# A linear-attention block with a GEGLU feed-forward: K^T V formed from tokens^T phi(K), and folded into the output weights

## The chip, the cores and the metric

The kernel runs on one core of a Trainium2 chip. The metric is device time in microseconds (us), as the median of several runs. All activations and weights are bf16, matmuls accumulate in f32 in PSUM (8 banks of 512 f32 a partition).

## What is computed

One token block of 2048 tokens, model width 448, 16 heads of 28, feed-forward width 1792 (a batch of one):

```python
def _A_ref(x, wqkv, wo):                      # x is layernorm(tokens)
    q, k, v = (x @ wqkv) split in three, 16 heads of 28
    phi = lambda t: jnp.where(t > 0, t + 1, jnp.exp(t)) + 1e-6
    pq, pk = phi(q), phi(k)
    kv = jnp.einsum("bhsd,bhse->bhde", pk, v)
    z = jnp.einsum("bhsd->bhd", pk)
    num = jnp.einsum("bhqd,bhde->bhqe", pq, kv)
    den = jnp.einsum("bhqd,bhd->bhq", pq, z)[..., None] + 1e-6
    return (num / den) put back to [S, 448] @ wo
...
h = x + _A_ref(_layernorm(x), A_wqkv, A_wo)
h2 = h + (gelu(n @ w_gate) * (n @ w_up)) @ w_down      # n = _layernorm(h)
```

## The kernel before

The 2048 tokens are 16 tiles of 128. A small graph class collects tasks (one task is one engine instruction or one run of matmuls) with the buffers that they read and write; from these it derives the semaphore waits. The order of the tasks on each engine is not found at run time: `ORDERS` is a table of five lists of task numbers (TensorE, ScalarE, VectorE, GpSimd, and SyncE with the DMAs that it issues). Each engine works through its list strictly in order, so a task that waits holds up all that stand behind it on its engine.

**First layernorm.** For each tile VectorE computes `bn_stats` and `bn_aggr` (L421, L422), ScalarE the reciprocal deviation as exp(-0.5 ln(var)) (L431, L433), and the normalised tile `xn` comes from VectorE (tiles 0 and 1, L458) or GpSimd (the rest, L461). It is transposed to `xnT` on TensorE for tiles 0 to 3 (L483 to L486), and by DMA transposes on SyncE's queue for tiles 4 to 15 (L494). Width 448 is three blocks of 128 rows and one of 64; the 64 are doubled by a copy (L467), so that the half block can be used from both halves of the array.

**K, V and the state.** Tiles go in pairs. K and V of a tile are three matmuls each over 128 rows (L513, L521) and one each over 64 rows; the two half matmuls (L524, L525) run at once in the two halves of the array. phi(K) takes three steps: ScalarE's exp out of PSUM (L539), GpSimd's clamp (L545), VectorE's max-and-add out of PSUM (L547). ScalarE copies V out (L549). Then four matmuls per tile (L555), 113 columns each, add phi(K)^T V in PSUM, four heads to a group, with a column of ones for z. After the last tile VectorE masks the blocks off the diagonal (L566, L567) into `kvz`.

**Q.** It is made transposed, 113 rows by 512 tokens at a time (L580, 16 pieces of four matmuls), and phi(Q) goes the same way: L583 on ScalarE, L584 on GpSimd, L585 on VectorE.

**Attention out, `a2_tile`.** Per tile: four matmuls give numerators and denominators at once (`nd`, L603); VectorE takes the reciprocals (L606) and multiplies (L607) into `o_sb`; that is transposed (tiles 0 and 1 on TensorE, L617; then DMA, L622); the output projection (`wo`, L630; in pairs L640 with two half matmuls L641, L642); VectorE adds the residual (L651); the second layernorm follows, with GpSimd's power (L438, L440) and normalisation (L665) from tile 2 on; the wide copy (L685); and the transposes to `hnT` (L675 on TensorE for tiles 0 and 1, then DMA, L686).

**Feed-forward.** `gu_chunk` takes 2, 2, 4, 4 and 4 tiles. Gate and up are 64-row matmuls in the two halves of the array, side by side (L741, L743), seven to a column block; ScalarE applies gelu (L765), VectorE multiplies (L767). `b2_tile` does the down projection, 14 matmuls per tile (L702), and VectorE adds the residual (L707). Gate uses PSUM banks 0 and 1, up 6 and 7, down 2 and 3, so that a gate/up step can run two ahead of VectorE and no more. There are 56 such steps, called gu0 to gu55 below; the first is issued when both tiles of the first chunk have their `hnT`. The order lists put the attention of tiles 4 and later between the gate/up steps, and the last Q pieces between the steps of the chain that leads to the first gate/up.

Of the kernel before, what the change touches and what calls it, by code (L numbers as in the profile page):

```python
# [5 lines left out]
BF16 = mybir.dt.bfloat16  # L6
F32 = mybir.dt.float32
ALU = mybir.AluOpType
AF = mybir.ActivationFunctionType

ENGS = ("pe", "act", "dve", "pool", "sp")
SEM_LAT = {"pe": 0.05, "act": 0.05, "dve": 0.05, "pool": 0.12, "sp": 0.06}
DMA_ISSUE = 0.45
DMA_LAT = 1.6
T0 = 0.8
CONTEND = 3.9
DMA_BW = 300e3
MODE_SWITCH = 0.1
MODE_HYST_64 = 1.2
MODE_HYST_128 = 0.0  # L20
MODE_MIN_64 = 2.5

# [3 lines left out]
    "30 43 36 152 153 145 59 51 146 159 160 246 151 171 158 172 165 250 170 183 184 177 254 182 195 196 189 207 194 208 201"  # L26
    " 258 206 220 221 213 232 219 233 226 262 231 266 238 270 243 274 313 310 278 282 316 318 343 340 290 320 286 326 294 298"
    " 348 302 334 364 338 367 306 413 418 423 428 433 438 372 443 391 388 448 478 483 396 488 493 457 454 451 498 503 462 508"
    " 543 548 553 519 522 513 516 527 558 563 628 625 568 573 578 583 633 588 593 598 603 608 652 649 616 613 657 673 678 683"
    " 688 693 698 703 619 622 708 713 718 723 728 733 738 743 746 755 760 765 770 775 780 785 790 795 800 805 810 815 820 749"  # L30
    " 752 825 828 831 834 837",
    "3 5 6 7 29 33 34 40 41 56 57 48 49 157 66 67 52 60 150 154 147 79 80 161 166 164 247 169 118 92 105 93 106 181 176 178"
    " 173 251 119 131 132 190 185 188 255 193 197 200 202 205 218 214 212 259 209 225 215 222 230 227 234 237 239 263 242 267"
    " 271 275 279 283 317 319 291 287 324 325 295 299 330 331 303 335 307 412 416 414 421 419 424 426 431 429 436 434 441 439"
    " 444 446 479 481 486 484 491 489 494 496 501 499 506 504 509 511 546 544 554 549 556 551 559 561 564 566 571 569 576 574"
    " 581 579 586 584 591 589 594 596 601 599 609 606 611 604 676 674 679 681 684 686 691 689 696 694 704 699 701 706 711 709"
    " 714 716 721 719 726 724 731 729 739 741 736 734 756 758 763 761 768 766 771 773 778 776 783 781 788 786 793 791 796 798"
    " 801 803 808 806 811 813 818 823 816 821",
    "19 20 31 32 38 39 35 53 42 45 44 54 46 61 37 63 62 64 100 74 87 115 69 113 76 75 72 77 114 156 88 101 149 116 89 102 82"
    " 85 128 90 103 163 249 168 108 126 95 98 127 129 175 253 111 180 187 192 124 121 137 199 257 204 134 211 217 224 229 261"  # L40
    " 236 241 265 244 245 269 314 311 315 312 277 273 281 341 344 342 345 321 285 322 327 323 328 289 329 332 293 333 336 349"
    " 337 352 297 339 350 351 368 301 353 417 415 365 354 366 422 420 369 425 427 362 432 430 359 305 309 435 442 437 440 376"
    " 373 377 374 445 378 375 389 447 390 392 393 386 480 482 485 397 487 398 400 401 402 399 383 449 455 490 492 456 458 497"
    " 495 459 407 410 500 502 507 505 466 510 512 463 547 545 452 464 467 555 557 520 465 521 523 524 552 550 517 528 531 529"
    " 532 560 562 530 533 626 565 468 567 629 627 572 570 630 577 575 514 582 538 580 473 585 541 587 476 592 590 595 597 634"
    " 602 600 637 653 650 651 612 605 610 654 635 614 607 636 638 658 659 677 675 617 680 682 661 685 687 692 690 697 660 695"
    " 662 663 639 620 702 700 644 707 647 668 705 712 710 715 717 671 623 722 720 727 725 732 730 740 742 735 737 757 759 764"
    " 762 769 767 772 774 779 777 784 782 789 787 794 792 797 799 802 804 747 809 807 744 812 814 822 819 817 824 750 753 826"
    " 829 832 835 838",
    "16 18 24 25 23 27 0 21 17 22 55 47 28 58 50 65 68 71 26 155 148 78 81 84 167 162 248 91 104 107 94 97 117 179 174 252"  # L50
    " 110 130 136 191 123 186 120 133 256 198 203 216 260 210 223 228 235 240 264 268 272 276 280 284 288 292 296 300 308 356"
    " 357 304 355 361 358 380 381 379 385 382 404 405 403 409 406 535 534 470 469 536 540 471 472 537 475 641 642 665 640 664"
    " 666 646 667 643 670",
    "1 2 4 8 9 10 11 12 13 14 15 70 73 83 86 96 99 109 112 122 125 139 135 141 138 140 143 142 346 347 144 371 370 360 363"
    " 394 395 387 384 460 461 411 408 525 526 631 632 450 542 474 515 539 477 655 656 615 648 621 669 453 672 618 645 754 830"
    " 751 748 827 624 518 745 836 833 839",
)


class _Buf:  # L60
    __slots__ = ("name", "writer", "readers")

    def __init__(self, name):
        self.name = name
        self.writer = None
        self.readers = []

# [4 lines left out]


class _Graph:


    def __init__(self):
        self.all = []
# [131 lines left out]
def bass_sequential_preLN__linear_attn_block__glu_gated_geglu__prompt_kernel(  # L210
# [4 lines left out]
    T = S // 128  # L215
# [625 lines left out]
```

## Time and profile before

| what | value |
|---|---|
| median of 3 runs | 203.81 us (202.98 to 204.15) |
| span of the profiled execution | 201.6 us, 2.2 us less than the median; the page gives no other time of that execution |
| first K matmul | 8.57 us into the span |
| first gate/up matmul | 58.72 us |
| end of the last matmul | about 199.1 us |
| busy: TensorE, VectorE, ScalarE, GpSimd | 194.9, 119.4, 70.4, 53.0 us |
| granted TensorE clock, mean | 0.992 of full speed |
| DMA transposes | 12 of `xn`, 14 of `o_sb`, 14 of `hn`, median 2.5, 2.5 and 3.0 us from issue to landing |

How to read it. The busy time of TensorE is modelled: a matmul counts from its start to the end of its flow through the array, so neighbours overlap. What a run of matmuls costs is read from start to start in the timeline. The same holds in a smaller way for the other engines: a row says how long one instruction took, and a run of like instructions takes somewhat less each. A digit in the line of 40 slices is the busy share of a slice of 5.04 us in tenths.

### The profile page before, as it was taken

How to read it: one execution, taken by the hardware profiler on the slowest of the kernel's cores; microseconds unless marked ns; L12 is line 12 of the kernel's file. 1: busy time of each engine (PE TensorE's matmuls, PEld its weight loads, DVE VectorE, ACT ScalarE, POOL GpSimd, SP SyncE). 2: the span in 40 equal slices, each digit the busy share in tenths (PEclk: the TensorE clock that was granted, in tenths of full speed). 3: DMA queues.
4: the chain of work that ended last, by engine and by line, in shares of the span. 5: the costliest groups of instructions: out<-in, count | busy, mean ns of one | idle time of the engine just before them, and what ended most of it. 6: DMA issues, size and time to landing. Idle time of an engine off the chain costs nothing.

```text
span 201.6 us, 4406 instructions
## 1 busy us (share of the span) xinstructions
PE 194.9 (97%) x1684; PEld 110.4 (55%) x1684; DVE 119.4 (59%) x312; ACT 70.4 (35%) x191; POOL 53.0 (26%) x105
## 2 busy tenths in 40 slices
PE   7599999799999999999999999999999999999995
PEld 7245455356578767675544445456444545555554
DVE  2877653369997875946657666564553324573112
ACT  3257556366564312222213232043032224432000
POOL 8349994344416050500006300003600000000000
PEclk9979999999999999999999999999999999999999
DMA  6942425999980613260111285100078000000014
GB/s 187 364 78 54 81 53 116 141 262 280 181 300 19 121 37 72 59 134 3 26 26 29 51 162 72 49 2 3 0 138 117 0 0 3 0 0 3 23 62 143
DMA packets 38276, 17.39 MB, mean 86 GB/s; under 512 B 29808, under 2 KB 37360, under 8 KB 38256
## 3 DMA queue, kind: packets, MB, share of 16 engines
q1 hardware_dynamic: 36832, 14.71, 34.0%
q10 hardware_dynamic: 1424, 2.41, 4.3%
q8 instruction: 13, 0.21, 0.4%
q14 instruction: 7, 0.06, 0.1%
HBM read 8.66 MB, written 1.84 MB: 52 GB/s over the span
## 4 chain that ended last, share of the span: by engine, by line
PE 90%; DMA 5%; SPq 2%; issue 1%; DVE 1%; ACT 0%; DVEq 0%
PE ps L741 36%; PE ps L702 21%; PE ps L743 7%; PE ps L580 7%; PE ps L640 4%; PE ps L513 4%; PE ps L521 4%; DMA xnT<-xn 3%; DMA x_sb<-in_A_x_dram 2%; PE ps L603 2%; PE ps L524 2%; PE ps L555 1%; SPq L494 1%; PE ps L641 1%; PE ps L630 1%
## 5 line engine op out<-in xcount | busy, mean ns | idle before, releaser
L743 PE MATMUL ps<-hnT,wgu_sb 64*128 64x512 bf16 (+1 forms) x490 | 87.3, 334 | 0.0
L741 PE MATMUL ps<-hnT,wgu_sb 64*128 64x512 bf16 (+1 forms) x490 | 86.9, 334 | 0.0
L765 ACT ACTIVATE gl<-ps 128x256 bf16<-128x256 f32 x112 | 36.5, 382 | 86.9 <-PE ps L743 83.3
L767 DVE TENSOR_TENSOR hh<-ps,gl 128x256 bf16<-128x256 f32 x112 | 42.5, 416 | 38.7 <-ACT gl L765 37.8
L741 PEld LDWEIGHTS ps<-hnT,wgu_sb 64*128 64x128 bf16 x490 | 45.4, 94 | 29.0 <-issue 1.5
L743 PEld LDWEIGHTS ps<-hnT,wgu_sb 64*128 64x128 bf16 x490 | 43.5, 94 | 4.8 <-DVE hh L767 1.2
L702 PE MATMUL ps<-wd_sb,hh 128*128 128x448 bf16 (+1 forms) x238 | 43.6, 342 | 0.0
L702 PEld LDWEIGHTS ps<-wd_sb,hh 128*128 128x128 bf16 x238 | 22.7, 98 | 19.4 <-issue 1.3
L421 DVE BATCH_NORM_STATS2 st<-x_sb 128x6 f32<-128x448 bf16 x32 | 19.0, 614 | 3.5 <-DMA x_sb<-in_A_x_dram 3.4
L707 DVE TENSOR_TENSOR x_sb<-ps,x_sb 128x448 bf16<-128x448 f32 (+1 forms) x17 | 10.1, 594 | 18.2 <-PE ps L702 18.2
L438 POOL TENSOR_SCALAR ln<-mv 128x2 f32<-128x2 f32 x7 | 1.5, 219 | 64.5 <-DVE mv L422 64.5
L547 DVE SCALAR_TENSOR_TENSOR pk<-ps,tm 128x448 bf16<-128x448 f32 x16 | 9.8, 620 | 13.0 <-POOL tm L545 12.1
L580 PE MATMUL ps<-xnT,wq_sb 128*113 128x512 bf16 x64 | 16.2, 381 | 0.0
L584 POOL TENSOR_SCALAR tm<-e 113x512 bf16<-113x512 bf16 x16 | 9.7, 613 | 10.2 <-ACT e L583 8.9
L513 PE MATMUL ps<-wkv_sb,xnT 128*128 128x448 bf16 x48 | 11.2, 367 | 1.2 <-DMA xnT<-xn 1.0
L545 POOL TENSOR_SCALAR tm<-e 128x448 bf16<-128x448 bf16 x16 | 9.0, 566 | 10.2 <-ACT e L539 6.7
L583 ACT ACTIVATE e<-ps 113x512 bf16<-113x512 f32 x16 | 9.5, 603 | 5.4 <-PE ps L580 4.6
L521 PE MATMUL ps<-wkv_sb,xnT 128*128 128x448 bf16 x48 | 11.2, 367 | 0.0
L549 ACT ACTIVATE v<-ps 128x448 bf16<-128x448 f32 x16 | 8.8, 555 | 6.2 <-PE ps L525 4.1
L585 DVE SCALAR_TENSOR_TENSOR pqT<-ps,tm 113x512 bf16<-113x512 f32 x16 | 10.6, 678 | 0.0
L539 ACT ACTIVATE e<-ps 128x448 bf16<-128x448 f32 x16 | 8.3, 549 | 6.4 <-PE ps L525 6.2
L651 DVE TENSOR_TENSOR x_sb<-ps,x_sb 128x448 bf16<-128x448 f32 x16 | 9.7, 615 | 1.5 <-PE ps L642 1.5
(72 smaller groups left out, 160.7 us busy)
## 6 DMA issues: line engine op xcount, KB each, us to landing
out_dram<-x_sb SPq DMA_DIRECT2D x15, 112.0 KB, 1.8
wgu_sb<-in_B_w_up_dram ACTq DMA_DIRECT2D x1, 1568.0 KB, 11.3
wgu_sb<-in_B_w_gate_dram SPq DMA_DIRECT2D x1, 1568.0 KB, 14.8
wd_sb<-in_B_w_down_dram SPq DMA_DIRECT2D x1, 1568.0 KB, 9.4
x_sb<-in_A_x_dram SPq DMA_DIRECT2D x2, 448.0 KB, 6.2
wkv_sb<-in_A_wqkv_dram ACTq DMA_DIRECT2D x2, 336.0 KB, 3.8
x_sb<-in_A_x_dram SPq DMA_DIRECT2D x3, 224.0 KB, 5.0
wo_sb<-in_A_wo_dram SPq DMA_DIRECT2D x2, 336.0 KB, 10.1
```

The source lines that it names most:

```text
L421: op("dve", lambda e: e.bn_stats(st[:, t, :], src_ap), [b_src], [b_st[t]], "bnst%d" % t, 0.53, key, after=after)
L513: ins = e.matmul(ps[:, BK_K[t % 4], 0:D], xnT[:, k, t * 128:(t + 1) * 128], wkv_sb[:, k, 0:D], start=(k == 0), stop=False)
L521: ins = e.matmul(ps[:, BK_V[t % 2], 0:D], xnT[:, k, t * 128:(t + 1) * 128], wkv_sb[:, k, D:2 * D], start=(k == 0), stop=False)
L547: op("dve", lambda e, i=i, ie=ie, psK3=psK3: e.scalar_tensor_tensor(pk[:, i, :, 1:GP], psK3, EPS, tm1[:, ie, :].rearrange("p (g e) -> p g ...
L580: ins = e.matmul(psQ, wq_sb[:, k, g, 1:GP + 1], xnT[:, k, c * QCH:(c + 1) * QCH], start=(k == 0), stop=(k == 3))
L585: op("dve", lambda e, i=i, c=c, g=g, psQ=psQ: e.scalar_tensor_tensor(pqT[:, g, c * QCH:(c + 1) * QCH], psQ, EPS, tm2[:, i, :], ALU.max, AL ...
L702: ins = e.matmul(psO, hh[:, j, (t % HR) * 128:(t % HR + 1) * 128], wd_sb[:, j, c0:c1], start=(j == 0), stop=(j == NJ - 1))
L707: op("dve", lambda e, t=t, psO=psO, c0=c0, c1=c1: e.tensor_tensor(x_sb[:, t, c0:c1], psO, h_sb[:, t, c0:c1], ALU.add), bank(bk) + [b_h[t]] ...
L741: e.matmul(psG[:, jj * N:(jj + 1) * N], wgu_sb[A_, k, j * 128:(j + 1) * 128], hnT[A_, ka_, c0:c0 + N], start=(k == 0), stop=(k == 6))
L743: ins = e.matmul(psU[:, jj * N:(jj + 1) * N], wgu_sb[B_, k, j * 128:(j + 1) * 128], hnT[B_, kb_, c0:c0 + N], start=(k == 0), stop=(k == 6))
L765: G.add("act", lambda e, gi=gi, cs_=cs_, psG=psG: e.activation(gl[:, gi, cs_], psG[:, cs_], AF.Gelu_apprx_tanh), r=bank(BK_G[i]), w=[b_glh ...
L767: op("dve", lambda e, dst=dst, srcU=srcU, srcL=srcL: e.tensor_tensor(dst, srcU, srcL, ALU.mult), bank(BK_U[i]) + [b_glh], [b_ar[j_][t % HR ...
```

## The change

The attention part is rewritten, with a new order table; the feed-forward has the same instructions in another order, and the graph class loses its unused cost fields.

- V of the tokens is not formed. Per tile four matmuls (`fpt`) add tokens^T phi(K), a 512 by 448 matrix, in PSUM banks 4 to 7 over all 16 tiles. The stationary operand is the normalised tile itself, `xnn`, as it lies (tokens on the partitions); its last 64 columns are ones, so that 64 rows of the sum hold z. Afterwards `wv` times that matrix gives K^T V by head group (16 matmuls, `fkv`), VectorE masks it, and it is multiplied into the output weights (four matmuls `w2_0` to `w2_3`), each with a copy out of PSUM.
- K and Q are both made per tile in token layout by four matmuls of 128 rows and 448 columns (`proj`); the fourth block of `xnT` holds 64 rows of tokens and 64 of ones against weight rows that are zero.
- phi(K): ScalarE's exp, then the clamp (`ck`) and the max-and-add (`pk`), both on VectorE. phi(Q): ScalarE's exp (`eq`) and relu (`rq`), both out of PSUM; later VectorE clamps (`cq`) and adds (`aq`) in SBUF.
- The denominator is not a matmul any more: per tile phi(Q) times z (`t1`, on GpSimd but for tile 0), VectorE's sum by head (`dr`), the small add (`de`), the reciprocal (`rd`), and phi(Q) times it (`pn`). The scaled phi(Q) is transposed (tiles 0 and 1 on TensorE, then one DMA transpose per pair), and four matmuls of 112 rows per tile against the folded weights (`out`) give the projected attention at once.
- `xnn` is a ring of 6 tiles (16 before); the first transposes leave PSUM in two halves, one on ScalarE and one on VectorE; the loads of x are split over two queues, and the loads of `wv`, `wo`, gate and down weights stand behind the last transpose of `xnn` on SyncE's queue.

In the new order the first Q tiles (0 to 3) lie between the K tiles, and tiles 4 to 15 come after the last K tile. TensorE's list around the joint reads: `k_15 pt4_13 pt4_14 pt1_15 pt3_15 q_5 q_4 kv q_6 q_7 w2_3 w2_1 w2_0 w2_2 q_10 tro_0 q_11 tro_1 q_9 out_0 q_15 q_8 q_13 q_14 out_1 trh_0 trh_1 q_12 gu2_0`. VectorE's: `pk_15 z1 evpD_3 z0 evpD_2 t1d_0 cq_5 dr_0 dr_1 de_0 kvm de_1 rd_0 rd_1 pn_0 evwD_1 pn_1 dr_2 dr_3 de_2 evwD_3 de_3 rd_2 rd_3 pn_2 pn_3 cq_4 aq_5 hr_1 hr_0 ...` (`out_p` and `oT_p` are a pair of tiles, the rest one tile.)

```diff
-        op("dve", lambda e: e.memset(pk[:, :, :, 0:1], 1.0), [], b_pk, "pkones", 0.07)
...
-        for pair in PAIRS:
...
-            def fv(e, W, pair=pair):
...
-                    ins = e.matmul(ps[:, BK_K[t % 4], 0:D], xnT[0:64, 3, t * 128:(t + 1) * 128], wkv_sb[0:64, 3, 0:D], start=False, stop=True)
-                    ins = e.matmul(ps[:, BK_V[t % 2], 0:D], xnT[64:128, 3, t * 128:(t + 1) * 128], wkv_sb[64:128, 3, D:2 * D], start=False, stop=True)
...
-                op("pool", lambda e, ie=ie: e.tensor_scalar(tm1[:, ie, :], e1[:, ie, :], 1.0 + EPS, 0.0, ALU.min, ALU.max),
...
-                def fnacc(e, t=t, i=i):
...
+        def proj(e, W, t, bk, w):
+            ins = None
+            for k in range(4):
+                W(k)
+                ins = e.matmul(ps[:, bk, 0:D], xnT[:, t, k, :], w[:, k, :], start=(k == 0), stop=(k == 3))
+            return ins
...
+        def k_tile(t):
...
+            eks.append(act_exp(lambda e: e.activation(e1[:, i, :], psK, AF.Exp), [b_ps[bk]], [b_e1[i]], "ek_%d" % t))
+            op("dve", lambda e: e.tensor_scalar(e1[:, i, :], e1[:, i, :], 1.0 + EPS, 0.0, ALU.min, ALU.max), [b_e1[i]], [b_e1[i]], "ck_%d" % t)
+            op("dve", lambda e: e.scalar_tensor_tensor(pk[:, i, :], psK, EPS, e1[:, i, :], ALU.max, ALU.add), [b_ps[bk], b_e1[i]], [b_pk[i]], "pk_%d" % t)
+            groups = ((3, 0, 1, 2),) if t < T - 1 else ((3,), (0, 1, 2))
+            for cs in groups:
+                def fpt(e, cs=cs):
...
+                        ins = e.matmul(ps[:, BK_PT[c], 0:D], xnn[:, t % XN_R, c * 128:(c + 1) * 128], pk[:, i, :], start=(t == 0), stop=(t == T - 1))
...
+        def q_tile(t):
...
+            act_exp(lambda e: e.activation(eq[:, t, :], ps[:, bk, 0:D], AF.Exp), [b_ps[bk]], [b_eq[t]], "eq_%d" % t)
+            act_exp(lambda e: e.activation(pq[:, t, :], ps[:, bk, 0:D], AF.Relu), [b_ps[bk]], [b_pq[t]], "rq_%d" % t)
...
+        op("dve", lambda e: e.tensor_copy(zbc[B_, :], ps[B_, BK_PT[3], 0:D]), [b_ps[BK_PT[3]]], [b_z[1]], "z1")
+        op("dve", lambda e: e.tensor_copy(zbc[A_, :], zbc[B_, :]), [b_z[1]], [b_z[0]], "z0")
...
+                    ins = e.matmul(ps[0:GW, BK_KV, g * GW:(g + 1) * GW], wv_sb[:, c, g * GW:(g + 1) * GW], pt_sb[:, c, g * GW:(g + 1) * GW],
+                                   start=(c == 0), stop=(c == 3))
...
+            G.add("pe", lambda e, g=g: e.matmul(ps[0:GW, BK_W2[g], 0:D], kvm[:, g, :], wo_sb[:, g, :], start=True, stop=True),
...
+        def a2_pair(p):
...
+                op("dve", lambda e, t=t: e.tensor_scalar(eq[:, t, :], eq[:, t, :], 1.0, EPS, ALU.min, ALU.add), [b_eq[t]], [b_eq[t]], "cq_%d" % t)
+                op("dve", lambda e, t=t: e.tensor_tensor(pq[:, t, :], pq[:, t, :], eq[:, t, :], ALU.add), [b_eq[t], b_pq[t]], [b_pq[t]], "aq_%d" % t)
...
+                op(eng, lambda e, t=t, n=n: e.tensor_tensor(t1[:, n, :], pq[:, t, :], zbc[:, :], ALU.mult), [b_pq[t]] + b_z, [b_t1[n]], "t1%s_%d" % (eng[0], t))
...
+                op("dve", lambda e, n=n, i=i: e.tensor_reduce(den[:, i, :], t1[:, n, :].rearrange("p (h d) -> p h d", h=H), AX.X, ALU.add),
...
+                G.add("sp", lambda e, i2=i2: e.dma_start_transpose(pqnT[:, i2, :, :, :].rearrange("p n g t -> p (n g) t"),
+                                                                 pqn[:, i2, :, :, :].rearrange("p n g c -> p (n g c)")),
...
+                        ins = e.matmul(ps[:, BK_OUT[n], 0:D], pqnT[0:GW, i2, n, g, :], w2[:, g, :], start=(g == 0), stop=(g == NG - 1))
```

## The prediction

> **What bounds the kernel now.** I read the page's busy shares and slices first.
>
> ```profile
> PE 194.9 (97%) x1684; PEld 110.4 (55%) x1684; DVE 119.4 (59%) x312; ACT 70.4 (35%) x191; POOL 53.0 (26%) x105
> PE   7599999799999999999999999999999999999995
> DVE  2877653369997875946657666564553324573112
> PEclk9979999999999999999999999999999999999999
> ```
>
> TensorE is full from slice 2 on. VectorE is dense in one place, slices 9 to 11 (45 to 60 us): the joint between attention and feed-forward. The chain that ended last says the same:
>
> ```profile
> PE 90%; DMA 5%; SPq 2%; issue 1%; DVE 1%; ACT 0%; DVEq 0%
> ```
>
> So the time is TensorE's work plus few holes. The work is priced from start to start in the timeline of TensorE (columns: start, length, line, shape, count):
>
> ```profile
> 26.60 1.30 PE L513 MATMUL ps<-wkv_sb,xnT 128*128 128x448 bf16 x6
> 27.73 1.30 PE L521 MATMUL ps<-wkv_sb,xnT 128*128 128x448 bf16 x6
> 28.96 0.36 PE L524 MATMUL ps<-wkv_sb,xnT 64*128 64x448 bf16 x1
> ...
> 29.45 0.42 PE L555 MATMUL ps<-v,pk 128*113 128x113 bf16 x4
> ...
> 31.05 1.30 PE L521 MATMUL ps<-wkv_sb,xnT 128*128 128x448 bf16 x6
> ...
> 33.02 1.03 PE L580 MATMUL ps<-xnT,wq_sb 128*113 128x512 bf16 x4
> 33.88 0.37 PE L555 MATMUL ps<-v,pk 128*113 128x113 bf16 x4
> ```
>
> Six matmuls of 448 columns take 1.13 us: 0.189 each. A pair of tiles costs 2.85 us for K and V (26.60 to 29.45), of which about 0.2 is the change to half height and back. The state costs 0.21 to 0.25 a tile, a piece of Q 0.86. The same reading gives 0.76 for `wo` of one tile, 1.53 for a pair, 0.52 for `nd` of a pair among gate/up, 2.65 for a down tile and 1.515 for a gate/up step.
>
> VectorE, ScalarE and GpSimd are priced by the groups kept apart by shape (busy, mean ns of one):
>
> ```profile
> L547 DVE SCALAR_TENSOR_TENSOR pk<-ps,tm 128x448 bf16<-128x448 f32 x16 | 9.8, 620 | 13.0 <-POOL tm L545 12.1
> L539 ACT ACTIVATE e<-ps 128x448 bf16<-128x448 f32 x16 | 8.3, 549 | 6.4 <-PE ps L525 6.2 <-ACT v L549 0.2
> L685 DVE COPY hn<-hn 128x448 bf16<-128x448 bf16 x14 | 3.8, 284 | 0.6 <-POOL hn L665 0.5
> L461 POOL TENSOR_SCALAR xn<-x_sb,nm,rs 128x448 bf16<-128x448 bf16 x14 | 9.9, 716 | 1.8 <-ACT rs L433 1.3 <-ACT ln L431 0.2
> ```
>
> Queued back to back they take less: two of L547 in 1.16, four `bn_stats` in 2.17, two L767 in 0.76. So a 448-wide VectorE operation is 0.535 us, the gate/up product 0.345, a bf16 copy about 0.2, a 448-wide ScalarE read of PSUM 0.49.
>
> **Its own time.** The span is 201.6 us, 2.2 under the median of 203.81. I work on the span and add 2.2.
>
> **Matmuls ahead of the first gate/up.** Before, to 58.72 us: K and V 8 x 2.85 = 22.8, state 3.7, Q 16 x 0.865 = 13.8, `nd` of three pairs 1.3, `wo` of four tiles 3.0, transposes 2.6; sum 47.2. After: K, Q and fpt are 192 x 0.189 = 36.3; `fkv` is 16 like L555's at 0.053 = 0.85; the four `w2` 0.76; two pairs of `out` 3.0; transposes 2.1; sum 43.0. **-4.2 us**, all on the path, since TensorE is full there. The half block of 64 rows is now paid at full height, and that is in these numbers.
>
> **Matmuls among gate/up.** Five pairs of `nd` go, 5 x 0.52 = 2.6; `out` (8 x 0.189 = 1.51) takes the place of `wo` (1.53). In the two order lists the stays at full height between gate/up steps fall from 12 to 6, and the first gate/up matmul after a down tile costs 0.32 instead of 0.21: 0.1 to 0.2 a stay, 0.3 to 1.3 in all, 0.7 taken. **-3.3 us.**
>
> **The start.** Before, tile 0 is normalised at 5.64 us, but its transpose waits for tile 1, whose normalisation stands behind `bn_stats` of tile 2, and that waits for x until 6.46. In the new list tile 0 goes first; only its second half copy (`evxD_0`) stands behind that `bn_stats`. The first K can begin near 6.5 and end near 7.8, not 9.3. The rows also show the clock at half from about 9.1 to 12.5 us, after a thin stretch on TensorE; 1.7 us go there, and may or may not come back. **-0.8**, bounds -2.9 and +0.5.
>
> **The K stage.** A tile is now K plus fpt, 1.51 us on TensorE. VectorE has `bn_stats` and aggregate 0.62, `ck` 0.2 and `pk` 0.535: 1.36, close under it; GpSimd 0.93, SyncE one transpose of 1.2. From the end of K to fpt of the same tile there are exp 0.55, clamp 0.25, max-and-add 0.62 and hand-overs, 1.85 us, covered by four runs of 0.757; for the last tile by two only: +0.4. The ring of 6 lets tile t+6 be normalised only when fpt of tile t is done: 0.75 plus the transpose's 2.5 to landing, 3.6 with hand-overs, against 4.5 us until K wants it. Before, the last transposes landed after up to 5.0 us beside the big weight loads, and K waited 1.0; the up weights again start beside them: 0 to 2.5, +0.6 taken. **+1.0**, bounds 0 and +3.
>
> **The joint.** From the last fpt to the first gate/up, TensorE has 12 Q (9.1), `fkv` and `w2` 1.6, two pairs of `out` 3.0, transposes 1.25: 15.0 us. ScalarE has 24 reads for Q, eight copies and the layernorm, about 16 us. VectorE's list puts `t1d`, `dr` and `pn` of the first tiles in front of `kvm` and the copies `evwD`; added up in its order, z1 to `hr_1` is 10.4 us, and another 6.3 through `bn_stats`, `nhD` and the copies of `hnT`: 16.7. Before, the chain took 13.75 (44.97 to 58.72) and TensorE was full throughout. So some 1.5 us of hole appear. `wv` and `wo` are issued behind the last transpose; 336 KB took 3.8 us early and 10.1 beside the weights, so `fkv` could wait up to 2. **+1.3**, bounds -1 and +3.5.
>
> **VectorE under the first gate/up.** From gu0 until the last attention pair but two has its `out`, TensorE has 28 steps, three `out` and three down tiles: 54.9 us. VectorE's list there: 55 products x 0.345 = 19.0; 37 wide ones (`pn`, `dr`, `hr`, `bn_stats`, `fo`) x 0.535 = 19.8; 9 `aq`, between the copy's 0.2 and 0.535, 0.3 taken for two bf16 inputs = 2.7; 16 of `cq` and the wide copy x 0.2 = 3.2; 20 small at 0.14 and 8 at 0.09 = 3.5. Sum 48.2, 88% of the stretch, where before VectorE was busy 38.25 of 53.3. The products stand in that queue, and gate/up may run only two steps ahead. **+1.0**, bounds 0 and +6. GpSimd loses 32 clamps (18.7 us busy) and gains 15 `t1`, between 0.57 and 1.4 us each by L545 and two of L461; it is never the bound there.
>
> **Two rules against it.** `t1`, `aq` and `pn` now read two SBUF tensors, while GpSimd normalises. The Trainium skill (GPSIMD Engine Reference, Specifications) says GpSimd shares its SBUF interface with VectorE, with contention from instructions with two SBUF inputs; and (Performance versus the Vector engine) a two-input GpSimd operation takes about 2.6 cycles an element, an estimate of 0.97 us for 448. No row here shows either; by the page 15 `t1` are 14.6 us on GpSimd, less than the 18.7 that leave it, and the sum would stay. On relu: L539 shows a PSUM read on ScalarE at 0.549 against L547's 0.620 on VectorE. The skill's page ScalarE: Activation LUTs (Rules for kernel authors) wants relu on VectorE. By the rule VectorE would get 12 x 0.535 = 6.4 us more at the joint, where it is the longer queue, and the time would be about 205; the rows are followed.
>
> **The sum.** -4.2 - 3.3 - 0.8 + 1.0 + 1.3 + 1.0 = -5.0: span 196.6, time **198.8 us**. Its own range, with bounds combined as independent, is 196 to 201.5.
>
> **Rivals.**
> - *VectorE becomes the bound (slower).* If its operations cost their row means instead of the back-to-back rate, with `aq` at 0.615, the stretch is 55 x 0.416 + 37 x 0.615 + 9 x 0.615 + 16 x 0.284 + 20 x 0.243 + 8 x 0.163 = 61.9 us against 54.9: 7 us of holes in place of 1.0, and 52 operations at the joint, 0.05 more each, 2.6. Span 196.6 + 6 + 2.6 = 205.2, time 207.4. It decides from about 14% above my prices. For it: 88% in strict order. Against: slices 9 to 11 show VectorE at 9 with TensorE at 9. Half its size gives about 203.
> - *ScalarE bounds the joint.* At the row mean, 24 x 0.55 = 13.2, eight copies 4.3, layernorm 0.5: 18.0 us instead of 16.7: time 200.1, with late weights (2 us) 202.1. For it: Q leaves PSUM by two reads, and relu and exp share one queue. Against: ScalarE is busy 35%.
> - *No new holes and no half clock.* -4.2 - 3.3 - 2.9 = -10.4 without the three plus terms; half of those remaining, time 195.
> - The change does what it says: the lists hold no V matmuls and no `nd`.
>
> **How the numbers follow.** Forecast 0.46, ScalarE 0.18, fewer holes 0.15, VectorE 0.21. About 0.5%, 1.0 us, is what a measurement can tell from no change. Of VectorE's 0.21, 0.17 is slower than 204.8, 0.03 within, 0.01 faster; of ScalarE's, 0.02 within and 0.01 slower; the rest is faster: faster 0.77, same 0.05, slower 0.18. The range, 194.0 to 206.0, leaves out some 0.05 below and 0.13 above.
>
> **What would show it.** In the profile after: first gate/up at about 56.0 us (58.72 before); then some 140.6 us to the end instead of 142.9; TensorE matmuls of 448 columns still 0.189 start to start; VectorE at 8 to 9 from slice 9 to 20; waits of gate/up for VectorE's products short. The forecast is wrong if those waits add up to more than 3 us, if K waits for `xnT` or `fkv` for `wv`, or if the K stage takes more than 1.7 us a tile.

## The result, and the profile after

The change makes the kernel slower: 209.47 us (median of 4, 208.17 to 210.56) against 203.96 (202.98 to 204.15, 4 runs on the same chip), a ratio of 1.0279 with a 95% interval of 1.0209 to 1.0348. The forecast was 198.8, the range ended at 206. The profiled execution took 208.17, with a span of 206.4 us. Executions of one kernel can fall into a faster and a slower group, some per cent apart; ratios and intervals here are of the faster group alone.

The page of the changed kernel, in the lines that were shown of before: busy shares, two engines and the clock in 40 slices of 5.16 us, and the chain that ended last.

```profile
PE 192.0 (93%) x1572; PEld 109.3 (53%) x1572; DVE 136.9 (66%) x372; ACT 73.5 (36%) x207; POOL 49.8 (24%) x91
...
PE   7899990598899999999999999999999999999995
...
DVE  2899972149999999996976788746553414552422
...
PEclk9999997579999999999999999999999999999999
...
PE 70%; DVE 15%; DMA 9%; ACT 3%; issue 2%; POOL 0%; ACTq 0%; DVEq 0%; POOLq 0%
```

TensorE has a slice that reads 0 (31 to 36 us) and one that reads 5, and from there the clock reads 7, 5 and 7. Before, no slice behind the start read so low, and the clock read 9 there throughout. VectorE's share of the chain rose from 1% to 15%, DMA's from 5% to 9%. The timeline of TensorE at that place (start, length, line, shape, count, and in brackets the idle time before it and who ended it):

```profile
27.92 0.92 PE L395 MATMUL ps<-wk_sb,xnT 128*128 128x448 bf16 x4
28.68 0.92 PE L414 MATMUL ps<-pk,xnn 128*128 128x448 bf16 x4
29.43 0.92 PE L395 MATMUL ps<-wk_sb,xnT 128*128 128x448 bf16 x4
30.19 0.92 PE L414 MATMUL ps<-pk,xnn 128*128 128x448 bf16 x4
38.38 1.65 PE L395 MATMUL ps<-wk_sb,xnT 128*128 128x448 bf16 x4 [7.28 <-DMA xnT<-xnn]
39.83 1.70 PE L414 MATMUL ps<-pk,xnn 128*128 128x448 bf16 x4
41.32 1.70 PE L395 MATMUL ps<-wk_sb,xnT 128*128 128x448 bf16 x4
42.82 3.48 PE L414 MATMUL ps<-pk,xnn 128*128 128x448 bf16 x12
46.14 1.11 PE L395 MATMUL ps<-wq_sb,xnT 128*128 128x448 bf16 x5
```

Until 30.19 the K stage runs as forecast: K and fpt of a tile take 28.68 + 0.75 - 27.92 = 1.51 us, four matmuls 0.757, 0.189 each. Then K of tile 14 waits 7.28 us for its transposed tile. After the wait the clock is at half: four matmuls take 1.45 to 1.50 us. The granted clock is the number third from the right in these rows (window, its length, busy time of TensorE, its weight loads, VectorE, ScalarE and GpSimd, clock, DMA share, GB/s):

```profile
38.38:43.80 5.42, 5.42 (x15) 2.24 (x16) 1.51 (x5) 1.09 (x2) 0.00 (x0) 0.50 1.09 269
43.90:46.10 2.20, 1.99 (x10) 0.73 (x9) 1.03 (x3) 0.00 (x0) 0.00 (x0) 1.00 1.05 209
```

Some 5.5 us of work run at half clock, so about 2.7 us go. The 24 matmuls from 38.38 to 46.14 take 7.76 us, where 24 x 0.189 are 4.54; the remaining 0.5 us is the last tile, whose `fpt` waits for its phi(K) at full clock as well (the third experiment has it). Who is late is seen in the chain that ended last (start, length, what):

```profile
27.69 10.56 DMA xnT<-xnn
```

It is one DMA transpose, issued on SyncE's queue at 27.69. ScalarE's timeline shows what was issued just ahead of it:

```profile
27.37 0.66 ACTq L277 DMA_DIRECT2D wgu_sb<-in_B_w_up_dram  x1
```

The up weights (1568 KB) take 10.7 us, to about 38.0; the transpose of tile 14 lands at 38.25, and tile 15's takes 9.6. The answer on the tile `xnT` has all twelve, from issue to landing:

```profile
DMA to landing us min/median/max: 2.4/2.6/10.6
```

The other ten land in the usual time. Before, the up weights were issued at 37.45 us, 2.4 us *after* the last transpose, and the last two landed after up to 5.0.

What the DMA engines did in that time is in the packets that the profile records. One transpose is 544 packets (0.13 MB), most of 256 bytes; the up weights go in packets of 3.6 KB. The first row is the queue of ScalarE from 33 to 36 us, the second that of SyncE in the same time (packets, MB, share of the 16 engines):

```profile
q10 hardware_dynamic: 169, 0.61, 94.6%
q1 hardware_dynamic: 168, 0.04, 12.6%
```

and SyncE's queue from 25 to 27 us, with no load beside it:

```profile
q1 hardware_dynamic: 544, 0.13, 32.5%
```

From 32.5 us on the two queues go packet for packet, 56 a microsecond each, so that the small packets of a transpose get on no faster than the large ones of the load. When the load's packets end, at about 36.6, the rest of both transposes passes in some 1.5 us. From 28.8 to 32.5 the load has the engines nearly alone (98%), and the record has one transpose packet; why, stays open.

The stages, by the timeline (z1 is the first copy of VectorE behind the last fpt; the forecast has z1 at 56.0 - 16.7):

| us into the span | forecast | after | the good version, below |
|---|---|---|---|
| first K | 6.5 | 6.62 | 6.35 |
| z1 | 39.3 | 45.77 | 34.71 |
| z1 to first gate/up | 16.7 | 17.87 | 17.86 |
| first gate/up | 56.0 | 63.64 | 52.57 |
| first gate/up to the end | 140.6 | 142.8 | 143.6 |
| span | 196.6 | 206.4 | 196.2 |

The groups by shape for the new operations, first VectorE's (busy us, mean ns of one, idle time before):

```profile
L487 DVE TENSOR_TENSOR pqn<-pq,rd 128x448 bf16<-128x448 bf16 x16 | 10.6, 675 | 0.0
...
L483 DVE TENSOR_REDUCE den<-t 128x16 f32<-128x448 f32 x16 | 9.5, 604 | 0.0
...
L480 DVE TENSOR_TENSOR t<-pq,zbc 128x448 f32<-128x448 bf16 x1 | 1.0, 1039 | 0.0
```

and GpSimd's:

```profile
L480 POOL TENSOR_TENSOR t<-pq,zbc 128x448 f32<-128x448 bf16 x15 | 15.6, 1044 | 42.7 <-DVE zbc L443 18.6 <-DVE pq L476 12.7 <-DVE den L483 8.1
```

`pn` and the reduction were priced at 0.535 back to back, `t1` of tile 0 on VectorE as well; that one took 1.04. GpSimd's 15 `t1` take 1.044 each, inside the bounds of 0.57 to 1.4.

### The profile page after: what moved, and what is told of

Its sections match the earlier page's. It is cut to its first block, busy times and chain, and to the rows that moved or that the text cites. A ratio compares the mean times of both kernels' runs of the same rounds, so it can differ in the third digit from the quotient of the medians.

```text
span 206.4 us, 4206 instructions
## 1 busy us (share of the span) xinstructions
PE 192.0 (93%) x1572; PEld 109.3 (53%) x1572; DVE 136.9 (66%) x372; ACT 73.5 (36%) x207; POOL 49.8 (24%) x91
## 4 chain that ended last, share of the span: by engine, by line
PE 70%; DVE 15%; DMA 9%; ACT 3%; issue 2%; POOL 0%; ACTq 0%; DVEq 0%; POOLq 0%
PE ps L590 20%; PE ps L562 19%; PE ps L592 15%; PE ps L395 6%; DMA xnT<-xnn 5%; PE ps L511 5%; PE ps L414 4%; DVE hh L612 3%; DMA x_sb<-in_A_x_dram 2%; DVE den L483 2%; DMA pqnT<-pqn 2%; DVE st L339 1%; DVE pqn L487 1%; DVE eq L475 1%; DVE pq L476 1%
## 5 line engine op out<-in xcount | busy, mean ns | idle before, releaser
L480 POOL TENSOR_TENSOR t<-pq,zbc 128x448 f32<-128x448 bf16 x15 | 15.6, 1044 | 42.7 <-DVE zbc L443 18.6
L395 PE MATMUL ps<-wk_sb,xnT 128*128 128x448 bf16 x64 | 16.2, 380 | 7.9 <-DMA xnT<-xnn 7.3
L566 DVE TENSOR_TENSOR x_sb<-ps,x_sb 128x448 bf16<-128x448 f32 (+1 forms) x17 | 10.1, 592 | 16.3 <-PE ps L562 16.3
L414 PE MATMUL ps<-pk,xnn 128*128 128x448 bf16 x64 | 16.0, 376 | 0.3
L395 PEld LDWEIGHTS ps<-wk_sb,xnT 128*128 128x128 bf16 x64 | 6.2, 103 | 15.2 <-issue 9.7
L395 PE MATMUL ps<-wq_sb,xnT 128*128 128x448 bf16 x64 | 13.9, 352 | 0.0
L511 PE MATMUL ps<-w,pqnT 112*128 112x448 bf16 x64 | 13.4, 353 | 0.2 <-DMA pqnT<-pqn 0.2
L407 DVE TENSOR_SCALAR e<-e 128x448 bf16<-128x448 bf16 x16 | 5.4, 338 | 11.5 <-ACT e L406 11.4
L343 POOL TENSOR_SCALAR nm<-mv 128x1 f32<-128x1 f32 (+1 forms) x19 | 4.2, 226 | 35.1 <-DVE mv L340 34.8
L545 POOL TENSOR_SCALAR hn<-x_sb,nm,rs 128x448 bf16<-128x448 bf16 x14 | 10.6, 764 | 0.5 <-POOL nm L343 0.2
L414 PEld LDWEIGHTS ps<-pk,xnn 128*128 128x128 bf16 x64 | 6.3, 104 | 8.3 <-issue 2.3
## 6 DMA issues: line engine op xcount, KB each, us to landing
wgu_sb<-in_B_w_up_dram ACTq DMA_DIRECT2D x1, 1568.0 KB, 10.7
wgu_sb<-in_B_w_gate_dram SPq DMA_DIRECT2D x1, 1568.0 KB, 16.7
```

The lines of the kernel that those rows point to most:

```text
L395: ins = e.matmul(ps[:, bk, 0:D], xnT[:, t, k, :], w[:, k, :], start=(k == 0), stop=(k == 3))
L414: ins = e.matmul(ps[:, BK_PT[c], 0:D], xnn[:, t % XN_R, c * 128:(c + 1) * 128], pk[:, i, :], start=(t == 0), stop=(t == T - 1))
L480: op(eng, lambda e, t=t, n=n: e.tensor_tensor(t1[:, n, :], pq[:, t, :], zbc[:, :], ALU.mult), [b_pq[t]] + b_z, [b_t1[n]], "t1%s_%d" % (eng ...
L511: ins = e.matmul(ps[:, BK_OUT[n], 0:D], pqnT[0:GW, i2, n, g, :], w2[:, g, :], start=(g == 0), stop=(g == NG - 1))
L545: op("pool", lambda e, t=t, sh=sh: e.tensor_scalar(hn[:, sh, 0:D], x_sb[:, t, :], nm2[:, t:t + 1], rs2[:, t:t + 1], ALU.add, ALU.mult), [b ...
L566: op("dve", lambda e, t=t, psO=psO, c0=c0, c1=c1: e.tensor_tensor(x_sb[:, t, c0:c1], psO, x_sb[:, t, c0:c1], ALU.add), [b_ps[bk], b_x[t]], ...
```

## The experiments

Theory A: a DMA transpose that is issued while a big load is under way lands only with that load, even when the load is on another queue; the price is what is left of the load. Theory B: the order or the ring of six normalised tiles makes tile 14 late, or another bound of the K stage is only covered by the hole. Line numbers in experiments with a changed order table are 30 lower than in the changed kernel (L365 for L395).

### The up weights later

```diff
 ScalarE's list:
-... ek_11 dwu ek_12 ek_13 ek_14 ...
+... ek_11 ek_12 ek_13 ek_14 dwu ...
```

> The load of the up weights moves on ScalarE's list from behind ek_11 to behind ek_14, nothing else. Theory A (the last two transposes of xnn land only when the up weights, issued just ahead of them on the other queue, have landed): the 7.3 us wait of k_14 falls under 1 us, the clock does not fall to half, the first gate/up comes at 53.5 us (52 to 55) in place of 63.6, time 199 us (197.5 to 201). Theory B (the new order or the ring of 6 makes the last tiles late): k_14 still waits, time 208 to 210.

Measured: 199.36, 202.52, 203.87 and 204.13 us. The profiled one is the slowest (span 202.4). The hole is gone: no transpose takes more than 3.5 us, K of tiles 14 and 15 start at 34.28 and 35.79. But this execution lost 3.3 us at the start (x of tile 2 landed at 8.5 us, not 6.5), and it shows the next thing that a late load holds up, in the timeline of TensorE:

```profile
45.97 0.94 PE L433 MATMUL ps<-wo_sb,kvm 112*112 112x448 bf16 x4 [2.15 <-DMA wo_sb<-in_A_wo_dram]
```

`wo`, issued at 34.79 beside 3136 KB of gate and up weights, took 11.0 us to land. Theory A holds for the hole, and the fastest run is at the 199 us expected; three of the four are 3 to 5 us above it, and what the kernel would give without the hole was still hidden by the start (in the profiled one) and by `wo`.

### The old kernel with its up weights early

```diff
-    dma(..., "dwu", D * FF * 2, after=[ek], q="act")
+    dma(..., "dwu", D * FF * 2, after=[], q="act")    # ScalarE's list: behind evv9
```

> The kernel before, with the up weights issued some 6 us earlier on ScalarE's list, behind evv9, so just ahead of the last two or three transposes of xn. Theory A: the pair of tiles 12 or 14 waits for xnT until about 42 us, 4 to 9 us of hole, part of it at half clock after that; time 208 to 214. Theory B: no change, 203.5 to 205.

Measured: 211.97 us, ratio 1.0399 [1.0356, 1.0441], inside the 208 to 214 of theory A. The up weights were issued at 29.54, and the old kernel got the same hole:

```profile
41.85 2.42 PE L487 MATMUL ps<-wkv_sb,xnT 128*128 128x448 bf16 x6 [7.73 <-DMA xnT<-xn]
```

Four transposes took 12.0, 11.1, 10.4 and 7.2 us, and landed 1.8 to 4.5 us behind the load; six matmuls behind the hole took 2.2 us instead of 1.13. The hole is no property of the new dataflow: it goes with the place of the load. Theory B falls.

### The hole filled

```diff
+for _ in range(34):     # ahead of K of tile 14: 34 matmuls of 512 columns on data that is there
+    e.matmul(ps[:, bk, 0:512], ones_bf[:], <xnT of tile 0>, start=True, stop=True)
```

> The changed kernel with 34 matmuls of 512 columns (7.3 us) on data that lie ready, put in front of k_14 into its own PSUM bank and overwritten by it, so that TensorE works through the hole. If the half clock behind the hole costs what the starts say (4.5 us of matmuls took 7.7), the fpt of the last tile ends 3.2 us earlier and the time is 206 us (205 to 207). If the half clock only delays what the joint would have waited for anyway, 209 to 210.

Measured: 207.08 us, ratio 1.0151 [1.0099, 1.0203], just above the 205 to 207 expected and far from 209 to 210; TensorE's timeline:

```profile
30.94 7.50 PE L408 MATMUL ps<-xnT,ones_bf 128*128 128x512 bf16 x34
38.28 0.92 PE L395 MATMUL ps<-wk_sb,xnT 128*128 128x448 bf16 x4
39.04 0.92 PE L422 MATMUL ps<-pk,xnn 128*128 128x448 bf16 x4
...
43.35 1.68 PE L395 MATMUL ps<-wq_sb,xnT 128*128 128x448 bf16 x8
```

K of tile 14 starts as late as before (38.28), but the four matmuls take 0.76 us again, and first gate/up comes at 60.88, 2.8 us earlier than 63.64. The same 24 matmuls take 5.07 us (38.28 to 43.35) in place of 7.76. The half clock is a price of its own, 2.7 us, on top of 7.3 us of waiting.

### The load in two parts

```diff
-dma("act", wgu_sb[B_, :, :],   B_w_up[...],        [b_wu],  "dwu",  after=[eks[11]])
+dma("act", wgu_sb[B_, 0:3, :], B_w_up[0:192] ...,  [b_wu],  "dwu",  after=[eks[11]])   #  672 KB
+dma("act", wgu_sb[B_, 3:7, :], B_w_up[192:448] ..., [b_wu2], "dwu2", after=[eks[14]])   #  896 KB
```

> The changed kernel with the up weights in two loads: 3 of 7 blocks (672 KB) behind ek_11 as before, 4 of 7 behind ek_14. Theory A with a price by bytes: xT_14 lands some 4.6 us after its issue in place of 10.6, k_14 waits 1 to 2 us, no half clock, time 200 to 202. Theory B: 208 to 210. If the order alone counts and the size does not: the wait stays near 7 us.

Measured: 202.0 to 203.5 us in three runs and 205.2 to 208.1 in seven; the three give a ratio of 0.9928 [0.9872, 0.9984]. In the profiled one (207.57, one of the seven) the first part takes 5.8 us, the last transposes at most 6.0, and K of tile 14 waits 2.60 us; 1 to 2 and no half clock were expected, and here 3.4 us of work behind the hole ran at half. The price goes by the bytes: 1568 KB took 10.7 us and the transpose 10.6; 672 KB took 5.8 and the transpose 5.2 to 6.0. A transpose that waited for a fixed reason would have stayed at 10.

### Loads of the V and output weights first, then x first

Two steps, on top of the first experiment's order (up weights behind exp of tile 14), as in all kernels from here to the put-back issue. In the first the loads of wv and wo move from behind the last transpose to the end of the first loads; in the second x of tiles 2 and 3 goes ahead of the last rows of the K weights, and x of tiles 4 and 5 ahead of the Q weights.

```diff
 SyncE's list (first step):
-... dx12 xT_4 ... xT_15 dwv dwv_t dwo dwg ...
+... dx12 dwv dwv_t dwo xT_4 ... xT_15 dwg ...
 second step, ScalarE:  -dx1 dwk_t dx2 dwq_t            +dx1 dx2 dwk_t dwq_t
              SyncE:    -dx0 dwk dwq dx4 dx6 ...        +dx0 dwk dx4 dwq dx6 ...
```

> Up weights issued behind exp of K tile 14 as in e1_up_later; the V and output weights (784 KB) are moved from behind the last transpose to the end of the first loads, ahead of the first transpose. Theory A (a load or transpose lands only with what big weight loads are under way when it is issued): with the 3136 KB of gate and up weights not yet issued they land by about 15 us, the 2.15 us wait of the w2 matmuls for wo and the half clock of some 4 us behind it (about 2 us lost) go: first gate/up 4 us earlier than e1_up_later's 58.99 at the same start, 55, or 52 if tile 2's x lands at 6.5 as in the changed kernel; time 197 to 200. Rival (VectorE's list is the bound of the joint, 16.7 us and more from the last fpt): the wait for wo only covered it, first gate/up comes at most 1 us earlier, time 202 to 203. Second rival: 784 KB ahead of the transposes delay the first of them and K waits for tile 4 or 5, 1 to 4 us lost.

> e5_vo_early with the first loads in another order: x of tiles 2 and 3 ahead of the last rows of the K weights on ScalarE's queue, x of tiles 4 and 5 ahead of the Q weights on SyncE's. If the place in the queue sets when x of tile 2 lands (6.5 us in the changed kernel, 8.5 in e1_up_later), it lands by 6.0, K tile 0 is done near 7.5 and no half clock follows at 10 to 12.5 us: 0 to 3.3 us less than e5_vo_early, time 195 to 198. If all early loads share the bandwidth whatever their order, tile 2's x still lands between 6.5 and 8.5 and the time is that of e5_vo_early within 1 us. If the rows of the K weights become late instead, K tile 0 waits for wk and the time is up to 1 us longer.

Measured: 209.09 us (208.27 to 209.72), ratio 1.0201 [1.0143, 1.0260], for the first step, and 204.64 (203.46 to 205.27), ratio 0.9985 [0.9953, 1.0018], for both. The first expectation missed, since the move brought in a wait that it did not see. SyncE's own timeline in the second kernel (start and length of the issues):

```profile
4.75 11.78 SPq L247 DMA_DIRECT2D wv_sb<-in_A_wqkv_dram  x2
```

and TensorE's in the same kernel:

```profile
21.12 1.22 PE L365 MATMUL ps<-wk_sb,xnT 128*128 128x448 bf16 x4 [4.62 <-DMA xnT<-xnn]
```

The load `dwv_t` writes 64 rows beside padding that GpSimd clears, and it waits for that clearing, which stood far down GpSimd's list, at 15.47 us. SyncE waited there until 16.5, and all transposes behind it on the queue with it: a hole of 4.6 us instead of 7.3, at tile 4. The wait for `wo` went as expected. The order of the first loads is worth 4.45 us between the two kernels, more than the 0 to 3.3 expected; the first fpt comes at 12.55 instead of 15.62. The 195 to 198 us expected of both steps were missed for the same wait on SyncE.

### GpSimd and VectorE at the joint

On top of the last kernel, `t1` of tiles 1 to 3 goes to VectorE; in another kernel the reduction reads 4 of a head's 28 columns.

```diff
-eng = "dve" if t == 0 else "pool"
+eng = "dve" if t < 4 else "pool"
```
```diff
-t1[:, n, :].rearrange("p (h d) -> p h d", h=H), AX.X
+t1[:, n, :].rearrange("p (h d) -> p h d", h=H)[:, :, 0:4], AX.X
```

> e6_x_first with the products t1 of tiles 1, 2 and 3 on VectorE instead of GpSimd (only tile 0's was there). Contention theory: VectorE's 1.04 us for t1 of tile 0, 0.62 for an add of 16 columns (0.16 elsewhere), 1.25 for pn (0.61 elsewhere) at the joint are due to GpSimd's two-input t1 running at the same time; with t1 on VectorE they fall to 0.62, 0.16 and 0.62, the three added t1 cost 0.535 each, and VectorE's list from z1 to hr_0 is as long as before within 0.5 us; time the same within 0.5%. Rival (t1 is slow by itself, fp32 operands): four t1 at 1.04, VectorE's list 3 us longer, and the time up to 3 us longer.

> e6_x_first with the sum for the denominator taken over 4 of a head's 28 columns: it leaves out 24 of 28 terms, and is there only to take work off VectorE: 16 reductions of 0.60 us become about 0.15, 7 us less, 1.8 of it at the joint, 5 in the first 70 us of gate/up. If VectorE is what makes the gate/up stage 142.8 us instead of the predicted 140.6, the stage falls by 1 to 2 us, and the joint by up to 1.8: time 1 to 3.5 us under e6_x_first. If those stretches are set by TensorE (price of out, changes of height), the stage stays within 0.4 us and the time within 0.5.

Measured: 205.74 us (204.89 to 206.51) and 203.93 (202.99 to 204.50), beside 204.64 without either; against the kernel before, the ratios are 1.0061 [1.0023, 1.0098] and 0.9956 [0.9921, 0.9990]. VectorE's timeline at the joint, first with `t1` on GpSimd:

```profile
44.15 1.04 DVE L450 TENSOR_TENSOR t<-pq,zbc 128x448 f32<-128x448 bf16 x1
...
46.96 0.62 DVE L455 TENSOR_SCALAR den<-den 128x16 f32<-128x16 f32 x1
...
47.78 1.24 DVE L457 TENSOR_TENSOR pqn<-pq,rd 128x448 bf16<-128x448 bf16 x1
```

then with the four `t1` on VectorE:

```profile
44.33 0.62 DVE L450 TENSOR_TENSOR t<-pq,zbc 128x448 f32<-128x448 bf16 x1
...
47.26 0.16 DVE L455 TENSOR_SCALAR den<-den 128x16 f32<-128x16 f32 x1
...
47.63 0.61 DVE L457 TENSOR_TENSOR pqn<-pq,rd 128x448 bf16<-128x448 bf16 x1
```

The same instructions fall from 1.04 to 0.62, from 0.62 to 0.16 and from 1.24 to 0.61 us: they were slow because GpSimd's product ran beside them. The Trainium skill (GPSIMD Engine Reference, Specifications) names contention with VectorE instructions that have two SBUF inputs, or run in a 2-port mode. `t1` and `pn` have two, and their rows agree; the 16-column add has one, and whether it runs in such a mode no run here shows. The three added products eat the gain: z1 to first gate/up is 18.20 against 17.85, and the time 0.5% longer, about as expected.

The short reduction takes 5.5 us off VectorE over the kernel (136.4 to 130.9 busy). At the joint it gives 1.0 us (16.87 against 17.85): VectorE's list bounds that part. In the gate/up stage, where VectorE was busy 97% from 60 to 80 us in the changed kernel, it gives 0.1 (143.36 against 143.47): less work on VectorE shortens that stage hardly at all. Two of its three waits for VectorE's products, shown further below, stayed at 0.4 to 0.5 us each.

### The good version, its joint in another order, and the one issue put back

The padding of wv is cleared at the start of GpSimd's list. Then, as two separate changes to that kernel, VectorE's list at the joint is put in another order, and the up weights go back behind exp of tile 11.

```diff
 GpSimd's list:   -... mones ... mask_a wvpad ...       +... mones wvpad ... mask_a ...
 VectorE (joint): +z1 evpD_3 z0 evpD_2 t1d_0 dr_0 kvm de_0 dr_1 de_1 rd_0 pn_0 rd_1 evwD_1 pn_1 evwD_3
                  +dr_2 ... pn_3 cq_5 hr_0 hr_1 ... nhD_1 wr64_1 aq_4 evhD_1 cq_6 aq_6 dr_4 de_4 hr_3
 ScalarE (put back): -... ek_14 dwu ...                 +... ek_11 dwu ...
```

> e6_x_first with GpSimd's clearing of the V weights' padding rows moved to the start of its list (it is idle there from 2.5 to 9.4 us). In e6_x_first SyncE stood from 5 to 16.6 us at the load of the last V rows, which waits for that clearing (at 15.47 us), and the transposes behind it came late: K tile 4 waited 4.62 us, and the half clock behind the hole took another 1.7 us. If that is all, first gate/up comes 6.3 us earlier than e6_x_first's 59.73, at 53.4, and the time is 198.3 (197 to 199.5): then the change itself, with its transposes not beside the up weights and its loads in order, is some 6 us under the kernel before. Rival: VectorE, ScalarE or the ring of six bounds the K stage (1.36 us a tile on VectorE against 1.51), the hole only covered it, and the time stays above 201.

> e9_pad_early with VectorE's list at the joint in another order: the copies of the folded output weights and the first pair's denominators first, and five operations that the first gate/up doesn't need (clamp, add and reduction of later tiles, residual of tile 3: 1.64 us by their rows) behind the copy of hnT. Theory (from z1 to the first gate/up, 17.85 us in four profiles, VectorE works without a gap and sets the end): it becomes about 16.2, where TensorE's 15.0 us of work are the next bound, and the time falls by 1 to 1.6 us under e9_pad_early. Rival: the moved operations stand in front of the first products and gate/up waits for them instead; time the same within 0.5 us. Second rival: TensorE or ScalarE sets the joint, 17.85 stays.

> e9_pad_early with the up weights back where the change puts them, behind exp of K tile 11 and so ahead of the last transposes: nothing else differs. Theory A: those transposes land only with the 1568 KB, K tile 14 waits 7 us as in the changed kernel, the clock goes to half behind it (2.5 to 3.4 us more), and the time is 197.84 + 10 = 207.5 to 208.5: then this one issue is the whole distance between the changed kernel and its good version. Rival (the start and the late loads of the V and output weights had their own part in the loss): the hole costs 5 us or less here, time 203 or less.

The good version: **197.84 us** (197.43 to 198.20), ratio 0.9697 [0.9647, 0.9747], faster than both kernels. Its page:

```profile
PE   7899999979999999999999989999999999999994
...
DVE  2999967999999999878867877555536214553412
...
PEclk9999999999999999999999999999999999999999
```

No hole, no half clock, no transpose of `xnT` over 3.7 us. First gate/up at 52.57 (53.4 expected), and the time inside the 197 to 199.5 expected.

The new order at the joint missed: 201.75 us (201.68 to 202.10), ratio 0.9894 [0.9854, 0.9934], 3.9 slower than the good version. z1 to first gate/up is 17.76, no shorter: `pn` of tile 3 comes 11.2 us behind z1 as before (11.3), and behind it TensorE's list has `out` of the second pair ahead of the transposes for the first gate/up, so VectorE now waits 1.1 us for TensorE. And the moved operations stand in front of the first products, as the rival had it (though it expected the time to stay); the waits of TensorE from 50 to 60 us:

```profile
PE ps L562 <- DVE hh L582: 2.1, 1, 2.1
PE ps L481 <- DMA pqnT<-pqn: 0.5, 1, 0.5
```

The wait of 2.1 us brought half clock from 59.25 to 62.67, 1.7 us more; from first gate/up to the end it is 147.0 against 143.6. In the profiled execution 0.9 us had been lost at the first fpt already (12.61 against 11.69).

The one issue put back: 207.85 us (207.09 to 208.49), ratio 1.0164 [1.0114, 1.0213], 10.0 us more than the good version, with nothing else changed, as theory A had it (207.5 to 208.5). The hole is there again:

```profile
37.80 1.65 PE L365 MATMUL ps<-wk_sb,xnT 128*128 128x448 bf16 x4 [7.16 <-DMA xnT<-xnn]
```

First gate/up is at 63.28, 10.7 us later than 52.57; 0.6 of it was there at the first fpt already (12.32 against 11.69).

### The same cure for the old kernel

```diff
 ScalarE's list of the kernel before:
-... evv12 dwu ek12 evv13 ek13 ek14 evv14 ek15 ...
+... evv12 ek12 evv13 ek13 ek14 evv14 ek15 dwu ...
```

> The kernel before with the same cure: its up weights moved from behind exp of K tile 12's pair (issued at 37.45 us, 2.4 us after its last transpose) to behind exp of K tile 15. If the up weights cost the kernel before nothing, because they are issued behind its transposes already, the time stays within 0.5% of 203.84, and what e9_pad_early gained belongs to the change and its start. Rival: the 1.0 us that its K tiles wait for a late transpose is of the same kind and goes: 202.8.

Measured: 206.23, 210.29, 210.69 and 210.75 us, too unequal for a ratio; both theories missed, and the fastest is still 2 us over the kernel before. The profiled one is the slowest. The up weights were issued at 42.51 and took 16.3 us, to 58.8. The attention's transposes `oT` were issued from 51.34 on; the slowest took 8.0, and the output projection waited:

```profile
59.44 2.40 PE L611 MATMUL ps<-wo_sb,oT 128*128 128x448 bf16 x6 [4.48 <-issue]
```

The profile names no releaser here; the landing time of `oT` (59.35) and the end of the load (58.8) fit theory A, with the next set of transposes in place of the last. A load moved away from one set of transposes must not end under the next.

## Why the prediction was wrong

**The step that failed** is the K stage: "the up weights again start beside them: 0 to 2.5, +0.6 taken". It cost 7.3 us of waiting, and 2.7 more at half clock, which the step did not have at all: 10.0, four times the upper bound. I had taken the 5.0 us landing of the old kernel's last transposes as the price of the big weight loads beside them. But there both were issued after these transposes. What ran beside them was `wo`, 336 KB, on SyncE's own queue (start, length; the second row is the chain's):

```profile
32.52 0.58 SPq L353 DMA_DIRECT2D wo_sb<-in_A_wo_dram  x1
33.20 5.05 DMA xnT<-xn
```

This `wo` took 5.1 us to 37.7, the transpose behind it 5.05 to 38.25: the effect in small, with 336 KB. In the new lists 1568 KB are issued ahead of two transposes. For tile 15 that was to be read off the lists: `dwu` stands behind exp of tile 11, the last transposes wait for the ring; that of tile 14 was issued only 0.3 us behind the load. What was missing was a row with a transpose behind a 1568 KB load; from the rows at hand an upper bound was about the load's own 11.3 us less what had run. The signs named beforehand were the right ones ("if K waits for `xnT`").

**The half clock.** The trace of before had it at 9.1 to 12.5 us "after a thin stretch on TensorE". I used it for the start only, and did not give the same price to the hole that I allowed in the K stage. The Trainium skill (TensorE: Matmul & The Clock Gate, Part 1) has half clock after an idle window of about 3.4 us and full clock after about 3.4 us of work. Half clock is seen here; full clock came back after 5.5 us of work. In the other runs holes of 2.1 us (new order at the joint) and 2.6 us (load in two parts) brought it too, for 3.4 us of work, so here shorter holes than the page's idle window were enough.

**What held.** 0.189 us a matmul and 1.51 a tile; the good version has z1 at 34.71, 4.6 us earlier than the forecast's 39.3, where the clock at the start stays up (bound -2.9, -0.8 taken, 2.1 more) and the +1.0 of the K stage is not paid; that makes some 3 of the 4.6, and the rest was not traced. In the changed kernel, 45.77 less 7.3 and 2.7 is 35.8, which is 3.5 earlier than forecast.

**The joint** was 17.87, not 16.7. VectorE sets it from z1 to `pn` of tile 3, at 57.1 us. From there the chain that ended last runs through the DMA transpose of that pair and then through TensorE's list (`out` of the pair from 60.47, and the transposes for the first gate/up):

```profile
57.11 3.22 DMA pqnT<-pqn
```

The prediction added up VectorE's list to the end, and that list alone does not bound the second part. In the first part its prices were too low in the contention with GpSimd: `t1d` 1.04 for 0.535, an add of 16 columns 0.62 for about 0.1, `pn` 1.24 for 0.535. The prediction had the rule and said that no row showed it; it should have put bounds on it.

**The gate/up stage** was 142.8, not 140.6. TensorE's timeline after, one pair of `out` and the gate/up matmul that follows:

```profile
70.40 1.69 PE L511 MATMUL ps<-w,pqnT 112*128 112x448 bf16 x8
72.02 0.28 PE L590 MATMUL ps<-hnT,wgu_sb 64*128 64x256 bf16 x1
```

and of the kernel before, one pair of `wo`:

```profile
68.20 1.31 PE L640 MATMUL ps<-wo_sb,oT 128*128 128x448 bf16 x6
...
69.64 0.27 PE L741 MATMUL ps<-hnT,wgu_sb 64*128 64x256 bf16 x1
```

`wo` took 1.44, `out` 1.62, where I had both at 1.5; over the stage a pair takes 1.58 against 1.44, and six pairs are 0.8 us. The five pairs of `nd` gave 2.2 back (0.45 each), not 2.6. Gate/up and down took 0.2 more than before, where 0.7 less was forecast for the fewer changes of height. And three gate/up steps start late, since their weight load waits for a product of VectorE (weight loads of TensorE, idle time before in brackets):

```profile
67.24 0.09 PEld L592 LDWEIGHTS ps<-hnT,wgu_sb 64*128 64x128 bf16 x1 [0.42 <-DVE hh L612]
86.55 0.09 PEld L592 LDWEIGHTS ps<-hnT,wgu_sb 64*128 64x128 bf16 x1 [0.56 <-DVE hh L612]
89.89 0.09 PEld L592 LDWEIGHTS ps<-hnT,wgu_sb 64*128 64x128 bf16 x1 [0.38 <-DVE hh L612]
```

They cost 1.1 us, close to the +1.0 of the forecast. So the 2.2 are 0.8 + 0.4 + 0.9 + 0.1.

**The sum.** 196.6 + 7.3 + 2.7 - 3.5 + 1.2 + 2.2 = 206.5, against a span of 206.4 measured. The agreement is no test of its own, since the -3.5 is a difference of the same times. The prediction's "196 to 201.5" for its bounds does not come out of them: combined as independent (root of the summed squares) they give some 195.3 to 204.8, and 209.47 lies outside that too.

**The rivals.** VectorE as the bound gave nearly the right time (207.4) for the wrong reason: it was to lose its 7 us in the gate/up stage, and lost about 1.2 at the joint. ScalarE did not bound the joint: VectorE works without a gap from z1 to `pn` of tile 3. "No new holes and no half clock" is the good version, forecast at 195, measured at 197.84, with its loads in another order. So the nearness of 197.84 to 198.8 is partly chance: a better start against a longer joint and gate/up stage.

## What to carry to other kernels

List what is issued, on all queues, in the time in which DMA transposes run: a big load issued ahead of a transpose costs that transpose about the rest of the load. In the old kernel with its up weights early, the slowest transpose took 1.5 us more than the whole load, so the load's duration is a guide and no bound. Add half clock to a hole on TensorE: holes of 2.1 to 7.7 us cost 1.7 to 3.0 us more here. When a load is moved, look at what it waits for and at the transposes that come next, since both moved the hole here instead of closing it.

## What the runs showed of the hardware that was not expected

- A transpose on SyncE's queue lands with the load on ScalarE's queue: 10.6 us with 1568 KB (10.7), 5.2 to 6.0 with 672 KB (5.8), 7.2 to 12.0 in the old kernel; alone 2.4 to 2.6. The Trainium skill (DMA: Bandwidth & Descriptors, Issuing engines are not separate DMA queues) says that DMAs of different engines share the 16 DMA engines and interleave. The packets agree: 169 of the load and 168 of the transposes from 33 to 36 us. But with packets of 256 bytes beside packets of 3.6 KB an equal share of packets is a small share of the bytes, so the transposes end with the load or behind it. A plain load with short rows fared the same: `wo`, in packets of 896 bytes, took 11.0 us beside the up weights in the first experiment.
- After a hole of 2.6 us (the load in two parts) the first four matmuls still ran at full clock, 0.75 us, and the next four took 1.44: the clock fell after the work had begun again (at 38.97 us; the work at 38.17). In all runs half clock lasted 3.41, 6.83 or 10.24 us, one, two or three times 3.41, but for the last microseconds of a kernel.
- GpSimd's two-input product of 448 columns, 1.04 us, stretched VectorE's instructions beside it by about 0.4 to 0.6 us each, a 16-column one from 0.16 to 0.62.
